# The last 64 rows of two weight matrices, loaded as two halves instead of one interleaved load

## The chip, the core and the metric

The kernel runs on one core of one Trainium2 chip. A core has a matrix engine (TensorE, PE in the profile; its weight loads are listed as PEld), three engines for vectors and scalars (VectorE or DVE, ScalarE or ACT, GpSimd or POOL), a SyncE (SP) that issues transfers here, and 16 DMA engines that carry them out. On-chip memory (SBUF) has 128 partitions. The metric is the device time of one execution in microseconds (us), median of several runs. Before the change it is 1147.22 us (3 runs, 1147.13 to 1147.64).

## The reference

Two kinds of layer alternate, A B A B, on eight batch rows of one token each, with D = 448 features:

```
A: q = norm(x) @ wq                       # wq: 448 x 4096, 16 heads of 256
   scores = q k^T / 16, softmax over 4096 keys, o = p v   # 8 kv heads, two q heads each
   x = x + o @ wo                         # wo: 4096 x 448
B: y = norm(x)
   x1 = y + shift(gelu(norm(y) @ w1)) @ w2
   x = x + x1 + gelu(norm(x1) @ w3) @ w4  # w3: 448 x 1792, w4: 1792 x 448
```

The shift moves features along the token axis; as there is one token, all that it moves in is padding, so its term is zero and w1 and w2 are never read. Both A layers read the same weights and the same caches. k_cache and v_cache are bf16 of 8 x 8 x 4096 x 256, 2 MB for each batch row and head, in all 128 MiB each.

## The kernel before, in words

**Tiling.** Weights stay in SBUF through the whole kernel. The contraction over D = 448 rows is cut into blocks of 128, 128, 128 and 64 rows, one block on the partitions at a time. The block with 64 rows is *packed*: its columns 0 to n/2 lie on partitions 0 to 63, its columns n/2 to n on partitions 64 to 127, so that it takes n/2 columns of SBUF in place of n (`packed`, lines 402 to 409; `packed_ap`, line 426, finds a column again). The right-hand side of the product has the last 64 features once on partitions 0 to 63 (slot 3) and once, copied in line 478 or 894, on 64 to 127 (slot 4), with zeros on the other half. `packed` is called for wq (line 411, n = 4096, 8 KB rows) and for w3 (line 533, n = 1792, 3.5 KB rows). wo and w4 have one load each (lines 530 and 534); w4's pieces are rows of 448 numbers.

**K and V.** SBUF has 30 slots of 4 KB on each partition for K and V (512 KB a slot). A K load fills two slots (1 MB; line 666), a V load one (line 741). DVE transposes K in place in 32-bit blocks (line 672), PE makes the scores (line 688), DVE, POOL and ACT the softmax (lines 696 to 722), PE the product with V (PV, line 752), and after a small transpose and combination (lines 757 to 774) PE multiplies by wo (line 782). With the last head of a batch row comes its `tail`: residual, two norms, w3 (line 810), gelu, w4 (line 835), residual, and in layer 0 the norm and q projection for the second A layer (line 492).

**Order.** The first A layer of batch row b runs next to the second of row b - 1. Some K blocks are kept in their slots from the first to the second (`KEPT`; for row 0 nine K loads, 18 of the 30 slots), and all other K and all V are read twice. The order of transfers is written by `load_order`; all of them are issued by SP, in one queue: x, then wq, then K and V of row 0 with wo after twelve K loads, then w3 and w4 after row 0's V, then row 1. `Graph.schedule` plays the kernel forward with durations and priorities given by hand, and with one modelled DMA queue of a fixed rate, and so fixes one static order for each engine. A semaphore stands for each slot and for each weight transfer; a consumer waits for those it needs. SP waits before an issue until the slot that it will fill is free; else it issues ahead.

**Where the change lies.** Lines 407 to 409: the fourth load of a packed weight. Its target is all 128 partitions, and its source is a view of the 64 rows with the half `u` as the first of three dimensions (2 x 64 x n/2). The first consumer of wq is the q projection of all eight rows at the start (PE, line 492, after `norm`, whose last instruction is line 478); of w3, the tail of row 0.

Of the kernel before, what the change touches and what calls it, by code (L numbers as in the profile page):

```python
# [6 lines left out]
P = 128  # L7
B = 8
D = 448
# [265 lines left out]
def bass_interleave_layers__gqa_block_cached__mixer_s_mlp__decode_kernel(  # L275
# [66 lines left out]
    def res(name, psum=False):  # L342
        if name not in R:
            R[name] = Res(psum)
        return R[name]
# [7 lines left out]
    def dma(fn, nbytes, prio, queue=dma_order, **kw):  # L353
        t = g.add("sp", fn, 0.0, prio, **kw)
        t.nbytes = nbytes
        queue.append(t)
        return t
# [44 lines left out]
    def packed(w_sb, w, n, name, queue):  # L402

        for c in range(3):
            dma(lambda e, c=c: e.dma_start(w_sb[:, c * n:(c + 1) * n], w[c * P:(c + 1) * P, :]),
                P * n * 2, 0, queue, writes=[res(name)])
        dma(lambda e: e.dma_start(w_sb[:, 3 * n:3 * n + n // 2],
                                  w[3 * P:D, :].rearrange("r (u f) -> u r f", u=2)),
            64 * n * 2, 0, queue, writes=[res(name)])

    packed(wq_sb, A_wq, HQ * DH, "wq", dma_order)

    def xin(e):
# [87 lines left out]
    def expand(layer, b, prio):  # L501
# [13 lines left out]
        for a in range(4):  # L515
            def cp(e, a=a):
# [14 lines left out]
                              A_wo.rearrange("(h m k) n -> m h (k n)", m=P, k=4)),  # L531
        D * 4096 * 2, 0, late, writes=[res("wo")])
    packed(w3_sb, B_w3, F, "w3", late)
    dma(lambda e: e.dma_start(w4_sb[:, 0:NFT * D].rearrange("p (t n) -> p t n", n=D),
                              B_w4.rearrange("(t m) n -> m t n", m=P)),
# [366 lines left out]
    for layer in range(2):  # L902
        d = {}
        for nm in ("n2", "n3"):
# [6 lines left out]
          writes=[res("xb0"), res("xb1"), res("xc0"), res("xc1")])  # L911
# [65 lines left out]
    for e in ("pe", "dve", "act", "pool"):  # L977
        n = 0
# [9 lines left out]
    for t in everything:  # L988
        e = t.chosen
# [94 lines left out]
```

## Time and profile before

| | us |
|---|---|
| median of 3 runs | 1147.22 |
| the profiled execution | 1147.47 |
| its span, first to last instruction | 1145.7 |
| DVE busy in the span | 770.8 (67%) |
| PE busy in the span | 700.3 (61%) |
| ACT, POOL busy | 114.5, 98.2 |

The span holds 41,855 instructions. DMA moves 452.63 MB, 395 GB/s over the span, almost all on the queue that SP issues to. 512 V loads and 163 K loads make nearly all of it.

A row of a table of stretches gives a stretch from A to B in us from the span's start, its length, the busy time (and number of instructions) of PE, PEld, DVE, ACT and POOL, the granted clock of PE as a share of full speed, the mean busy share of the 16 DMA engines (a little above 1 where transfers on one engine overlap), and the GB/s that they moved. A row in order of time gives start, duration, engine, line, operation, output <- input, and, in brackets, how long the engine had been idle and what ended that. For a DMA issued by SP (SPq), the duration is that of the issue on SP and not of the transfer.

### The profile page before, as it was taken

How to read it: one execution, taken by the hardware profiler on the slowest of the kernel's cores; microseconds unless marked ns; L12 is line 12 of the kernel's file. 1: busy time of each engine (PE TensorE's matmuls, PEld its weight loads, DVE VectorE, ACT ScalarE, POOL GpSimd, SP SyncE). 2: the span in 40 equal slices, each digit the busy share in tenths (PEclk: the TensorE clock that was granted, in tenths of full speed). 3: DMA queues.
4: the chain of work that ended last, by engine and by line, in shares of the span. 5: the costliest groups of instructions: out<-in, count | busy, mean ns of one | idle time of the engine just before them, and what ended most of it. 6: DMA issues, size and time to landing. Idle time of an engine off the chain costs nothing.

```text
span 1145.7 us, 41855 instructions
## 1 busy us (share of the span) xinstructions
PE 700.3 (61%) x18716; PEld 465.1 (41%) x18716; DVE 770.8 (67%) x2704; ACT 114.5 (10%) x434; POOL 98.2 (9%) x269
## 2 busy tenths in 40 slices
PE   0435465586556855577555775568555676557765
PEld 0322354244432544335443454335443355333553
DVE  2855589645995369943897449954699538974463
ACT  0100012101110011100111011100111001110110
POOL 0000011001110011100111001100111001110010
PEclk9999986557555565555555555555655555555655
DMA  9999899999999999999999999999999999999993
GB/s 300 415 386 371 309 401 415 411 403 407 414 414 399 403 415 415 412 398 397 414 415 408 402 407 415 414 400 401 416 414 413 396 399 416 414 407 403 405 407 150
DMA packets 101384, 452.63 MB, mean 395 GB/s; under 512 B 10948, under 2 KB 12884, under 8 KB 79956
## 3 DMA queue, kind: packets, MB, share of 16 engines
q1 hardware_dynamic: 101188, 449.96, 98.2%
q8 instruction: 146, 2.39, 0.9%
q14 instruction: 34, 0.28, 0.1%
q10 hardware_dynamic: 16, 0.01, 0.0%
HBM read 449.91 MB, written 0.01 MB: 393 GB/s over the span
## 4 chain that ended last, share of the span: by engine, by line
DMA 36%; DVE 35%; PE 20%; issue 7%; SPq 1%; ACT 1%; ACTq 0%; DVEq 0%
DMA kv<-in_A_v_cache_dram 30%; DVE kv L672 22%; PE psO L752 7%; PE psS L688 6%; DMA kv<-in_A_k_cache_dram 5%; DVE psX L711 2%; DVE small L696 2%; PE psM L492 2%; PE psM L782 2%; DVE oX L757 1%; DVE oT L771 1%; DVE small L884 1%; PE psO L764 1%; PE psM L810 1%; DVE small L698 1%
## 5 line engine op out<-in xcount | busy, mean ns | idle before, releaser
L672 DVE STREAM_TRANSPOSE kv<-kv 128x512 int32<-128x512 int32 x652 | 431.2, 690 | 32.8 <-DMA kv<-in_A_k_cache_dram 32.6
L688 PE MATMUL psS<-kv,qx 128*8 128x128 bf16 x8192 | 253.1, 295 | 178.6 <-DVE kv L672 83.0
L752 PE MATMUL psO<-kv,ring 128*2 128x256 bf16 x4096 | 290.2, 397 | 105.3 <-DMA kv<-in_A_v_cache_dram 89.5
L688 PEld LDWEIGHTS psS<-kv,qx 128*8 128x8 bf16 x8192 | 194.5, 114 | 238.2 <-DVE kv L672 113.1
L752 PEld LDWEIGHTS psO<-kv,ring 128*2 128x2 bf16 x4096 | 80.5, 93 | 180.5 <-DMA kv<-in_A_v_cache_dram 144.6
L757 DVE STREAM_TRANSPOSE oX<-psO 128x256 f32<-128x256 f32 x128 | 56.2, 439 | 110.2 <-PE psO L752 109.6
L700 POOL PARTITION_ALL_REDUCE small<-small x128 | 46.6, 364 | 726.2 <-DVE small L698 719.0
L782 PE MATMUL psM<-oT,wo_sb 128*128 128x1 bf16 x2048 | 74.3, 166 | 53.6 <-DVE oT L771 39.9
L706 ACT ACTIVATE psX<-psS,small 128x256 f32<-128x256 f32 x128 | 57.4, 448 | 455.3 <-DVE small L702 411.1
L696 DVE TENSOR_REDUCE small<-psS 128x1 f32<-128x256 f32 x128 | 52.4, 409 | 70.4 <-PE psS L688 53.3
L782 PEld LDWEIGHTS psM<-oT,wo_sb 128*128 128x128 bf16 x2048 | 64.1, 104 | 83.0 <-DVE oT L771 64.2
L771 DVE TENSOR_SCALAR oT<-psO,small 64x4 bf16<-64x4 f32 x256 | 55.4, 216 | 47.3 <-PE psO L764 42.7
L720 POOL PARTITION_ALL_REDUCE small<-small x128 | 51.4, 401 | 272.5 <-DVE small L718 237.8
L711 DVE STREAM_TRANSPOSE psX<-psX 128x256 f32<-128x256 f32 x128 | 57.6, 450 | 11.8 <-ACT psX L706 10.3
L764 PE MATMUL psO<-oX,id 128*32 128x4 f32 x1024 | 36.9, 201 | 28.1 <-DVE oX L757 21.2
L764 PEld LDWEIGHTS psO<-oX,id 128*32 128x32 f32 x1024 | 30.6, 147 | 46.0 <-DVE oX L757 36.6
L835 PE MATMUL psM<-small,w_sb 128*128 128x1 bf16 x896 | 30.1, 166 | 23.8 <-DVE small L827 23.7
L835 PEld LDWEIGHTS psM<-small,w_sb 128*128 128x128 bf16 x896 | 26.9, 104 | 38.6 <-DVE small L827 29.0
L715 ACT CAST ring<-psX 128x64 bf16<-128x64 f32 x128 | 27.2, 213 | 149.3 <-DVE psX L711 149.3
L492 PEld LDWEIGHTS psM<-small,wq_sb 128*128 128x128 bf16 x1024 | 30.7, 104 | 17.2 <-issue 12.0
L810 PE MATMUL psM<-small,w_sb 128*128 128x1 bf16 x896 | 28.8, 166 | 10.9 <-DVE small L894 6.7
L492 PE MATMUL psM<-small,wq_sb 128*128 128x1 bf16 x1024 | 34.2, 166 | 2.0 <-DVE small L894 1.8
(91 smaller groups left out, 354.1 us busy)
## 6 DMA issues: line engine op xcount, KB each, us to landing
kv<-in_A_v_cache_dram SPq DMA_DIRECT2D x512, 512.0 KB, 9.1
kv<-in_A_k_cache_dram SPq DMA_DIRECT2D x163, 1024.0 KB, 19.1
wo_sb<-in_A_wo_dram SPq DMA_DIRECT2D x1, 3584.0 KB, 27.9
wq_sb<-in_A_wq_dram SPq DMA_DIRECT2D x3, 1024.0 KB, 7.0
w_sb<-in_B_w_dram SPq DMA_DIRECT2D x1, 1568.0 KB, 21.3
w_sb<-in_B_w_dram SPq DMA_DIRECT2D x3, 448.0 KB, 15.3
wq_sb<-in_A_wq_dram SPq DMA_DIRECT2D x1, 512.0 KB
w_sb<-in_B_w_dram SPq DMA_DIRECT2D x1, 224.0 KB
```

Source lines behind the costliest of these rows:

```text
L492: last = e.matmul(M[:, base + col * nb:base + (col + 1) * nb], w, xn[:, :, kx], start=(k == 0), stop=(k == NCC - 1))
L672: return e.transpose(ap, ap)
L688: last = e.matmul(S[32 * j:32 * j + 8, w * y:w * y + w], qx[x][:, h, 2 * c + u, :], kt[:, :, c, 8 * j:8 * j + 8, u], start=(c == 0 and u = ...
L696: g.add("dve", lambda e: e.tensor_reduce(pm[par][:, :], S[:, 0:256], axis=AX.X, op=ALU.max), (0.46, 0.33), pr, reads=[rS], writes=[res(f"p ...
L706: g.add("act", lambda e: e.activation(p_ps.rearrange("p (z k y) -> p y z k", z=8, k=8), S[:, 0:256].rearrange("p (y z k) -> p y z k", y=4, ...
L711: g.add("dve", lambda e: e.transpose(p_ps, p_ps), (0.48, 0.38), pr, reads=[rP], writes=[rP])
L752: last = e.matmul(O[32 * j:32 * j + 2, 0:DH], ring[:, pin.slot, i, 2 * a:2 * a + 2], slot_ap(vin)[:, i * DH:(i + 1) * DH], start=(a == 0 a ...
L757: g.add("dve", lambda e: e.transpose(oX[:, :].rearrange("p (c r) -> p c r", r=32), O[:, 0:DH].rearrange("p (a r k) -> p a k r", a=2, k=4)) ...
L764: last = e.matmul(O[32 * a:32 * a + 32, 256:260], id4[:, :], oX[:, :].rearrange("p (a k r) -> p a k r", a=2, k=4)[:, a % 2, :, a // 2], st ...
L771: g.add("dve", lambda e, j=j: e.tensor_scalar(oT[64 * j:64 * j + 64, jb, 4 * h:4 * h + 4], O[64 * j:64 * j + 64, 256:260], rc_ring[64 * j: ...
L782: last = e.matmul(psM[layer][:, c:c + 1], wo_sb[:, c0:c0 + P], oT[:, jb, kt_:kt_ + 1], start=(first and k == 0 and c == 0), stop=False, sk ...
L835: last = e.matmul(M[:, 64 + c:65 + c], w4_sb[:, c0:c0 + P], hT[:, ft:ft + 1], start=(ft == 0), stop=(ft == NFT - 1))
```

## The change

The fourth load of each packed weight is taken apart by halves. Each of the two new loads brings 64 rows of n/2 columns to 64 partitions: the first to partitions 0 to 63, the second to 64 to 127. The same bytes go to the same places, in two issues of SP in place of one, each with its own semaphore. The planner sees two transfers of half the bytes. This is done for wq (256 KB each) and w3 (112 KB each).

```diff
         for c in range(3):
             dma(lambda e, c=c: e.dma_start(w_sb[:, c * n:(c + 1) * n], w[c * P:(c + 1) * P, :]),
                 P * n * 2, 0, queue, writes=[res(name)])
-        dma(lambda e: e.dma_start(w_sb[:, 3 * n:3 * n + n // 2],
-                                  w[3 * P:D, :].rearrange("r (u f) -> u r f", u=2)),
-            64 * n * 2, 0, queue, writes=[res(name)])
+        for u in range(2):
+            dma(lambda e, u=u: e.dma_start(w_sb[64 * u:64 * u + 64, 3 * n:3 * n + n // 2],
+                                           w[3 * P:D, u * n // 2:(u + 1) * n // 2]),
+                32 * n * 2, 0, queue, writes=[res(name)])
```

## The prediction

> **What bounds the kernel now.** I read the page first: the slices, the chain that ended last and the DMA issues.
>
> ```profile
> DMA  9999899999999999999999999999999999999993
> GB/s 300 415 386 371 309 401 415 411 403 407 414 414 399 403 415 415 412 398 397 414 415 408 402 407 415 414 400 401 416 414 413 396 399 416 414 407 403 405 407 150
> ...
> DMA 36%; DVE 35%; PE 20%; issue 7%; SPq 1%; ACT 1%; ACTq 0%; DVEq 0%
> ...
> wq_sb<-in_A_wq_dram SPq DMA_DIRECT2D x3, 1024.0 KB, 7.0
> w_sb<-in_B_w_dram SPq DMA_DIRECT2D x1, 1568.0 KB, 21.3
> ...
> wq_sb<-in_A_wq_dram SPq DMA_DIRECT2D x1, 512.0 KB
> w_sb<-in_B_w_dram SPq DMA_DIRECT2D x1, 224.0 KB
> ```
>
> The DMA engines are busy from the start to the last slice, at about 410 GB/s, except in slices 1 and 5 (300 and 309). A slice is 28.6 us: slice 1 holds the load of wq, slice 5 (114 to 143 us) follows that of w3. The last two lines are the two loads that the change splits; they alone among the weights have no time to landing.
>
> Then a table of stretches; its columns are start and end, length, busy time of the five engine rows, the clock, the DMA share and GB/s.
>
> ```profile
> 2.50:11.60 9.10, 0.00 (x0) 0.00 (x0) 1.36 (x13) 0.00 (x0) 0.52 (x3) 1.00 0.96 397
> 11.60:27.60 16.00, 1.54 (x8) 1.28 (x8) 4.13 (x27) 0.00 (x0) 0.62 (x3) 1.00 1.01 280
> 27.60:71.50 43.90, 20.52 (x600) 14.23 (x600) 34.83 (x86) 5.19 (x16) 3.40 (x9) 1.00 1.02 412
> 71.50:83.50 12.00, 3.24 (x80) 1.68 (x80) 6.24 (x17) 1.37 (x6) 1.16 (x3) 1.00 0.95 357
> 83.50:109.50 26.00, 12.58 (x320) 7.64 (x320) 13.51 (x31) 0.78 (x3) 0.76 (x2) 1.00 1.02 412
> 109.50:126.50 17.00, 7.41 (x134) 3.26 (x127) 8.46 (x42) 1.39 (x5) 0.76 (x2) 1.00 0.57 174
> 126.50:145.50 19.00, 9.85 (x322) 9.01 (x326) 13.09 (x46) 0.99 (x4) 0.54 (x2) 1.00 1.00 406
> 145.50:160.00 14.50, 9.30 (x300) 7.07 (x292) 11.44 (x34) 2.05 (x8) 1.33 (x4) 1.00 0.98 390
> 160.00:1130.00 970.00, 629.67 (x16834) 416.11 (x16828) 669.39 (x2371) 102.02 (x392) 88.59 (x235) 0.54 1.01 407
> 113.50:117.50 4.00, 2.44 (x48) 0.94 (x48) 0.88 (x3) 0.00 (x0) 0.00 (x0) 1.00 0.13 53
> ```
>
> From 160 us on nothing is left over: share 1.01 for 970 us, while DVE is busy 669 of 970 (69%) and PE 630 (65%). The end is therefore set by when the DMA engines get through their 450 MB. The last row is the key: for 4 us, 0.13 of 16 engines worked, that is two, at 53/2 = 26.5 GB/s each, the same as the 412/16 = 25.8 of one engine in the full stretches. Two engines had a backlog; fourteen had nothing.
>
> Last, the order of time around those stretches, and the end of the chain.
>
> ```profile
> 18.66 0.17 DVE L478 COPY w_sb<-w_sb 64x8 bf16<-64x8 bf16 x1
> 28.17 3.56 PE L492 MATMUL psX<-w_sb,wq_sb 128*128 128x8 bf16 x128 [12.34 <-DMA wq_sb<-in_A_wq_dram]
> 30.33 1.90 DVE L672 STREAM_TRANSPOSE kv<-kv 128x512 int32<-128x512 int32 x3 [11.49 <-DMA kv<-in_A_k_cache_dram]
> 109.26 8.41 SPq L534 DMA_DIRECT2D w_sb<-in_B_w_dram  x1
> 117.72 10.30 SPq L666 DMA_DIRECT2D kv<-in_A_k_cache_dram  x5
> 133.02 0.71 DVE L672 STREAM_TRANSPOSE kv<-kv 128x512 int32<-128x512 int32 x1 [4.03 <-DMA kv<-in_A_k_cache_dram]
> 137.20 0.33 SPq L666 DMA_DIRECT2D kv<-in_A_k_cache_dram  x1
> ...
> 1114.81 15.08 DMA kv<-in_A_v_cache_dram
> ```
>
> The normed input is ready at 18.83 us, yet the q projection starts at 28.17 (waiting for wq) and the first K transpose at 30.33. I read the backlog as the work of line 407: its source has the half (two of them) as its outermost dimension, and the load is dealt to two engines. The Trainium skill has that rule: DMA: Bandwidth & Descriptors, "Why a DMA increments its semaphore by 16 and not by 1", says that the engine count is the largest number up to 16 that divides the slowest dimension of both sides, so 2 here and 16 for a half with 64 rows; the trace agrees with the 2 (share 0.13), and no row of before shows the 16.
>
> **The change part by part.** *The wq load.* 512 KB (524,288 B) on two engines is 262 KB each, 262/25.8 = 10.2 us; on sixteen it is 524/412 = 1.3 us. Every K load behind it has a share on the two engines and lands only with them. Beyond this backlog all sixteen were slower while it ran: 280 GB/s over 16.0 us against 412 just after. Lost there: 16.0 x (1 - 280/412) = 5.1 us. That the load slows the others is inferred: the rate is 397 before it and 412 after it. From both sides: 0 to 5.1; I take 5.1, since the 412 follows with the same K loads in the queue.
>
> *The lag carried on.* At 71.5 to 83.5 engines run dry for want of issues: 12.0 x (1 - 357/412) = 1.6 us. I put it down to slots freed late because the two engines deliver late.
>
> *The w3 load and w4 behind it.* 224 KB on two engines is 115/25.8 = 4.4 us each, on top of what is left of the first lag. The issue of w4 stands 8.41 us in SP's queue, and five K loads another 10.3. That is the 0.13 row: w4's data has not begun, so I read SP's queue as held by the two engines' full rings. 174 GB/s x 17.0 us is 2.96 MB, of which w4 is 1.61. At 412 the rest, 1.35 MB, takes 3.3 us. For w4, whose rows are shorter (896 B), 412 GB/s gives 3.9 us; 313, measured at 120 to 124 us beside the w3 load, gives 5.1; I take 4.5 between them. Lost: 17.0 - 3.3 - 4.5 = 9.2 us (8.6 to 9.8).
>
> *What it adds.* Two issues in place of one for each weight. SP took 0.36 to 0.43 us for a wq block and 0.64 for the load that goes, so about 0.2 us more; behind it stand the first five K loads, whose data starts only when the engines finish wq at 11.6 us, so that 8 us of queue cover it. At w3, rings are full and an issue lasts as long as the drain. Each of the PE groups that waits for a weight gets one more semaphore to test, early in the kernel, with DMA as the bound: 0. The planner sees two tasks of half the bytes on one modelled queue, so the second ends when the one ended; I expect the order kept, slot numbers at most changed. POOL and ACT queues are not touched.
>
> *The price of a load to 64 partitions* no row shows. Nearest is the wq block to 128 partitions at 397 GB/s: cost 0. As if only half the engines' rate were to be had (206 GB/s), 524 + 229 KB cost 3.6 us in place of 1.8, so 1.8 more. A gain below 0 is excluded, as these bytes cannot go faster than the full stretches. Nothing decides, so I take 0.9. On this the Trainium skill speaks against the change: SBUF — State Buffer, "Door 1: The DMA port swizzle", says partitions 0 to 63 reach half of the sixteen ports; by its asymptote of 218 GB/s I estimate 1.6 us more, and no run here shows it.
>
> **Does the compute let it through?** After wq the first K would land at 11.6 + 1.3 + 2.5 (1 MB at 412) = 15.4 us, and DVE is free at 18.83, so the q projection and the transposes move 9 to 11 us up. Batch 0's last PV (117.83) waits on the two engines; it moves by 8.9 (10.2 - 1.3) + 5.1 = 14 us, to 104. From it to SP's next free slot (K load issued at 137.20) are 19.4 us, 4.0 of them DVE's wait for the late K: so 15.4, and the issue falls at about 119. The loads issued ahead of it (five K, two V, 6.3 MB, 15.3 us) follow w4, which would land at about 112 to 115, and last to 127 or later: the queue does not run dry. After that everything is the same sequence, earlier, with DMA still the bound and the same 16 us from the last V (1129.9) to the end.
>
> Sum: 5.1 + 1.6 + 9.2 - 0.9 = 15.0 us. The profiled execution took 1147.47 (span 1145.7, 1.8 around it): 1132.5; against the median of 1147.22, 0.25 less: 1132.2, say 1132. If the stretches from 126.5 to 160 also fill up (0.3 + 0.8), and 9.8 and 0 hold, the gain is 17.6; with 8.6 and 1.8 lost, it is 13.5. Own range 1129 to 1134.
>
> **The rivals.** *The slow start is K's own* (strided K rows at the start of a run): then 5.1 stays, the gain is 9.9, 1137.3. For it: the stretch holds K loads alone. Against: the rate is 412 from the instant that q projection can start. Chance 0.10.
>
> *Given back at the slots.* Kept K blocks fill 18 of 30 slots until layer 1 of batch 0. If its tail moves only as far as the first compute, 9.3 us (28.17 to 18.83), DMA runs dry before 160 us and the gain is 9.3: 1137.9. For it: SP's 8 us wait before 137.20. Against: the 15.4 worked out above, DVE at half load before 130. Chance 0.09.
>
> *Nothing changes:* two loads to separate halves run as late as one did; 1147.2. The same page of the Trainium skill, under "Can I just issue two DMAs to hit both halves?", says that they serialize; it speaks of sixteen engines on both sides, so what it would take is the 0.9 to 1.8 above, and the 0.13 row is against more. Chance 0.04.
>
> *Slower:* each half is dealt to one engine, and both to the same one. Then its backlog doubles, 20.3 and 8.9 us in place of 10.2 and 4.4: 14.6 more, 1161.8. It decides below two engines for a half; at two it is even. For it: no row shows a half. Against: all 128-partition loads ran on sixteen. Chance 0.03.
>
> **How the numbers follow.** The main case has 0.74. Measurements here tell 0.2% (2.3 us) from no change. Faster: 0.74 + 0.10 + 0.09 = 0.93; same 0.04; slower 0.03. The range 1128.5 to 1138 holds the main case nearly whole, with 0.5 us below for what later stretches may do, and both partial cases: about 0.85.
>
> **What would show it.** Right: the stretch 11.6 to 27.6 at about 410 GB/s; q projection near 19 us; first transpose near 19; no stretch with a DMA share of 0.13; w4 landed near 112 to 115; the last V near 1115; both halves with an ordinary time to landing. Wrong: 280 GB/s still there from 11.6 (the first rival), shares well below 1 between 115 and 160 with SP waiting on PE (the second), or the q projection still at 28 us (the third) or later (the fourth). A shift at 160 us that shrinks again by the end would say that DMA isn't the bound throughout.

## The result, and the profile after

The changed kernel takes 1133.5 us (median of 4 runs, 1133.38 to 1133.89) against 1147.18 us (4 runs, 1146.98 to 1147.64): a ratio of 0.9881, 95% interval 0.9864 to 0.9898, 13.7 us less. The profiled execution took 1133.89 us, its span 1132.1. The static order of every compute engine is the same as before; SP's list differs only in the two loads that became two issues each.

The page of the changed kernel, the slices and the DMA issues:

```profile
DMA  9999999999999999999999999999999999999993
GB/s 344 415 412 394 411 417 412 405 384 417 415 412 402 404 415 415 403 404 409 415 414 400 402 413 415 413 397 401 416 415 413 395 410 413 416 395 407 409 408 135
...
wq_sb<-in_A_wq_dram SPq DMA_DIRECT2D x2, 256.0 KB, 11.6
w_sb<-in_B_w_dram SPq DMA_DIRECT2D x2, 112.0 KB, 14.7
```

Slice 1 went from 300 to 344 GB/s and slice 5 from 309 to 411; slices 3, 4 and 6 rose too. From the seventh on they lie between 384 and 417 GB/s in both kernels, but for the last. The halves now have a time to landing (11.6 and 14.7 us).

The table of stretches of the changed kernel, columns as before (start and end, length, busy time of the five engine rows, clock, DMA share, GB/s):

```profile
2.50:11.60 9.10, 0.00 (x0) 0.00 (x0) 1.35 (x13) 0.00 (x0) 0.20 (x1) 1.00 0.98 370
11.00:15.00 4.00, 0.95 (x6) 0.78 (x6) 1.13 (x9) 0.00 (x0) 1.14 (x5) 1.00 1.01 225
11.60:15.60 4.00, 0.95 (x6) 0.78 (x6) 1.63 (x12) 0.00 (x0) 0.93 (x4) 1.00 1.00 257
11.60:27.60 16.00, 5.67 (x164) 5.24 (x168) 9.56 (x37) 1.80 (x3) 0.93 (x4) 1.00 1.01 376
27.60:71.50 43.90, 19.17 (x536) 12.14 (x524) 35.42 (x94) 4.75 (x18) 4.56 (x12) 1.00 1.02 413
71.50:83.50 12.00, 5.48 (x136) 3.39 (x136) 4.14 (x9) 0.00 (x0) 0.00 (x0) 1.00 1.02 414
83.50:105.00 21.50, 11.67 (x264) 5.89 (x264) 12.75 (x36) 2.16 (x8) 1.51 (x4) 1.00 1.02 410
105.00:115.00 10.00, 4.56 (x102) 3.16 (x102) 5.08 (x28) 0.00 (x0) 0.00 (x0) 1.00 1.07 372
115.00:130.00 15.00, 7.53 (x241) 6.78 (x241) 12.32 (x44) 0.78 (x3) 0.36 (x1) 1.00 1.01 418
160.00:1114.00 954.00, 618.19 (x16534) 410.01 (x16522) 654.57 (x2326) 99.56 (x382) 86.01 (x228) 0.54 1.02 408
```

No stretch has a low DMA share any more. The rate is below 400 only around the halves: 370 from 2.5 to 11.6 (397 before), 257 in the four microseconds after 11.6, and 372 at 105 to 115. The body, 408 GB/s at a share of 1.02, is as it was.

The changed kernel in order of time, and the last wait of its chain (the lines after the change are numbered one higher than before):

```profile
19.34 1.30 DVE L673 STREAM_TRANSPOSE kv<-kv 128x512 int32<-128x512 int32 x2
19.37 0.78 PE L493 MATMUL psX<-w_sb,wq_sb 128*128 128x8 bf16 x23 [3.06 <-DVE w_sb L479]
...
95.62 1.96 SPq L408 DMA_DIRECT2D w_sb<-in_B_w_dram  x2
97.62 0.85 SPq L535 DMA_DIRECT2D w_sb<-in_B_w_dram  x1
98.52 14.51 SPq L667 DMA_DIRECT2D kv<-in_A_k_cache_dram  x5
106.33 0.60 PE L753 MATMUL psO<-kv,ring 128*2 128x256 bf16 x8 [0.66 <-DMA kv<-in_A_v_cache_dram]
122.37 0.33 SPq L667 DMA_DIRECT2D kv<-in_A_k_cache_dram  x1
...
1099.98 16.34 DMA kv<-in_A_v_cache_dram
```

The q projection starts at 19.37 in place of 28.17, released by the norm (DVE, line 479) and no longer by wq; the first transposes start at 19.34 in place of 30.33. SP is through with w4's issue in 0.85 us in place of 8.41. Batch 0's last PV is at 106.33 (117.83 before), the late K issue at 122.37 (137.20), and the last V load's PV at 1099.98 + 16.34, 1116.3 (1129.9). So these events come 9 to 15 us earlier in the first 130 us, and 13.6 us are left at the end.

### The profile page after: what moved, and what is told of

It reads as the page before. It is cut to its first block, busy times and chain, and to the rows that moved or that the text cites. A ratio compares the mean times of both kernels' runs of the same rounds, so it can differ in the third digit from the quotient of the medians.

```text
span 1132.1 us, 41859 instructions
## 1 busy us (share of the span) xinstructions
PE 698.0 (62%) x18716; PEld 466.5 (41%) x18716; DVE 770.5 (68%) x2704; ACT 114.5 (10%) x434; POOL 98.3 (9%) x269
## 4 chain that ended last, share of the span: by engine, by line
DVE 35%; DMA 32%; PE 23%; issue 8%; ACT 1%; SPq 0%; POOL 0%; POOLq 0%; ACTq 0%; DVEq 0%
DMA kv<-in_A_v_cache_dram 28%; DVE kv L673 21%; PE psO L753 8%; PE psS L689 7%; PE psM L493 3%; DMA wo_sb<-in_A_wo_dram 2%; DVE psX L712 2%; DVE small L697 2%; PE psM L783 2%; DMA kv<-in_A_k_cache_dram 2%; DVE oX L758 1%; PE psO L765 1%; DVE oT L772 1%; DVE small L885 1%; PE psM L811 1%
## 5 line engine op out<-in xcount | busy, mean ns | idle before, releaser
L673 DVE STREAM_TRANSPOSE kv<-kv 128x512 int32<-128x512 int32 x652 | 431.1, 690 | 16.7 <-DMA kv<-in_A_k_cache_dram 16.4
L689 PEld LDWEIGHTS psS<-kv,qx 128*8 128x8 bf16 x8192 | 196.9, 115 | 243.8 <-DVE kv L673 118.4
L836 PEld LDWEIGHTS psM<-small,w_sb 128*128 128x128 bf16 x896 | 27.0, 104 | 37.7 <-DVE small L828 27.6
## 6 DMA issues: line engine op xcount, KB each, us to landing
w_sb<-in_B_w_dram SPq DMA_DIRECT2D x1, 1568.0 KB, 18.1
w_sb<-in_B_w_dram SPq DMA_DIRECT2D x3, 448.0 KB, 16.4
wq_sb<-in_A_wq_dram SPq DMA_DIRECT2D x2, 256.0 KB, 11.6
w_sb<-in_B_w_dram SPq DMA_DIRECT2D x2, 112.0 KB, 14.7
```

The lines of the kernel that those rows point to most:

```text
L673: return e.transpose(ap, ap)
L689: last = e.matmul(S[32 * j:32 * j + 8, w * y:w * y + w], qx[x][:, h, 2 * c + u, :], kt[:, :, c, 8 * j:8 * j + 8, u], start=(c == 0 and u = ...
L836: last = e.matmul(M[:, 64 + c:65 + c], w4_sb[:, c0:c0 + P], hT[:, ft:ft + 1], start=(ft == 0), stop=(ft == NFT - 1))
```

## The experiments

**Each load alone.** The two halves for wq only, and for w3 only:

```diff
-        dma(... one load, source "r (u f) -> u r f" ...)
+        if name == "wq":          # the other kernel: "w3"
+            for u in range(2):
+                dma(... half u to partitions 64 * u to 64 * u + 63 ...)
+        else:
+            dma(... one load, source "r (u f) -> u r f" ...)
```

> Only wq's last rows are loaded as two halves; w3 keeps the interleaved load. Theory (two engines carry the interleaved load, and the lag of wq's is still there when w3's comes): the slow start (5.1 us), the thin stretch (1.6) and the carried lag go; w3's own lag (4.4 us of work on two engines against 0.6 shared, 3.8 more) stays, so 5.4 of the 9.2 us at w4 go too. Half loads cost the 1.5 us that the changed kernel shows at 11.6 to 15.6 us. 1147.2 - 5.1 - 1.6 - 5.4 + 1.5 = 1136.6 us. Rival (the 9.2 us at w4 come from w3's load alone): 1147.2 - 6.7 + 1.5 = 1142.0, with a stretch of 0.13 DMA share as long as before.

> Only w3's last rows are loaded as two halves; wq keeps the interleaved load. Theory: the slow start and the thin stretch stay, the lag of wq's load is still there at 110 us, and only w3's own 3.8 us go, less 0.6 for two half loads: 1144.0 us; q projection at 28 us as before. Rival (the stall at w4 is w3's alone): all of 9.2 us goes, 1138.6.

Measured: wq alone 1134.4 us (ratio 0.9885, 0.9871 to 0.9900), w3 alone 1144.4 us (0.9974, 0.9964 to 0.9985), beside 1147.6. Expected were 1136.6 and 1144.0, so wq alone gave 2.2 us more than thought. The gains are 13.2 and 3.2; together they would make 16.4, and the change as a whole gave 13.7. The two loads share a loss: the 9.2 us at w4 need the lag that wq's load left. Stretches around w3 and w4, first of the kernel with wq's halves, then of the one with w3's:

```profile
105.00:110.00 5.00, 2.39 (x48) 0.91 (x40) 0.99 (x5) 0.00 (x0) 0.00 (x0) 1.00 1.05 370
110.00:115.00 5.00, 1.59 (x33) 1.43 (x34) 3.31 (x21) 0.00 (x0) 0.00 (x0) 1.00 1.00 285
97.22 7.37 SPq L540 DMA_DIRECT2D w_sb<-in_B_w_dram  x1
```

```profile
115.00:120.00 5.00, 2.90 (x48) 0.91 (x48) 0.84 (x3) 0.00 (x0) 0.00 (x0) 1.00 0.60 214
119.00:121.00 2.00, 0.84 (x19) 0.29 (x12) 0.89 (x3) 0.00 (x0) 0.00 (x0) 1.00 0.13 53
120.00:125.00 5.00, 1.73 (x30) 1.39 (x30) 2.46 (x16) 0.00 (x0) 0.00 (x0) 1.00 0.56 184
109.69 0.59 SPq L540 DMA_DIRECT2D w_sb<-in_B_w_dram  x1
110.33 13.79 SPq L672 DMA_DIRECT2D kv<-in_A_k_cache_dram  x5
```

With wq's lag gone, w3's interleaved load no longer empties the engines (share 1.00 at 110 to 115), although w4's issue still takes 7.37 us on SP. The stretch 105 to 115 moves 328 GB/s against 372 in the changed kernel, which is worth 1.1 us. The times differ by 1 us at most (1134.4 beside 1133.4 to 1134.2 in the runs of the changed kernel), and their intervals overlap, so the runs don't show that splitting w3 as well brought anything; I had left 3.8 us for it.

With wq's lag kept, a stall comes although w3 is split and w4 is issued in 0.59 us. From 119 to 121 us the share is 0.13 again, two engines at work alone. The only source left in this kernel whose outermost dimension is two is that of wq's load, issued at 2.5 us: its backlog is still there more than 100 us later. A long issue alone is not the sign of this. The five K loads stand in SP's queue for 13.79 us here and for 14.51 in the changed kernel, whose engines are busy all the while; what counts is whether fourteen engines run out of work meanwhile. So the stall comes from the backlog of wq's load, and it falls on whichever issue comes when the others are done. The rival that made w4's stall w3's own is refuted by both (1142.0 and 1138.6 expected).

**Four engines.** The same bytes in two loads whose sources have an outermost dimension of four:

```diff
+        for u in range(2):
+            dma(lambda e, u=u: e.dma_start(w_sb[:, 3 * n + u * n // 4:3 * n + (u + 1) * n // 4],
+                w[3 * P + 32 * u:3 * P + 32 * u + 32, :].rearrange("r (v f) -> v r f", v=4)), ...)
```

> The last 64 rows in two loads of 32 rows, each to 128 partitions, from a source whose outermost dimension is a quarter of the columns (four of them). The same bytes, but other numbers on the partitions than the products want, so that the projections by wq and w3 are not the reference's; nothing else is changed. Theory (the outermost dimension of the source sets the number of engines, here four): wq's backlog is 131 KB, 5.1 us an engine against 1.3 shared, w3's 2.2 against 0.6; the excess is 3.8 + 1.6 = 5.4 us against 8.9 + 3.8 = 12.7 before, and if the loss goes with it, 15.9 x 5.4/12.7 = 6.8 us are lost: 1147.2 - 9.1 = 1138.1. Rival (it is the one load with its 128 partitions and interleaved source, however dealt): as before, 1147; rival (the split in two issues is what helps): 1133.

Measured: 1140.1 us (0.9936, 0.9921 to 0.9951), a gain of 7.5 where 9.1 was expected. The stretches and the q projection of this kernel:

```profile
11.60:27.60 16.00, 5.40 (x152) 4.97 (x152) 8.10 (x34) 0.14 (x1) 0.68 (x3) 1.00 1.01 311
105.00:110.00 5.00, 2.94 (x55) 0.96 (x56) 1.92 (x7) 0.99 (x4) 0.40 (x1) 1.00 0.75 301
110.00:115.00 5.00, 2.59 (x54) 1.01 (x51) 0.89 (x3) 0.00 (x0) 0.00 (x0) 1.00 0.53 171
109.00:112.00 3.00, 2.13 (x40) 0.71 (x32) 0.44 (x2) 0.00 (x0) 0.00 (x0) 1.00 0.26 105
21.50 3.56 PE L493 MATMUL psX<-w_sb,wq_sb 128*128 128x8 bf16 x128 [5.59 <-DMA wq_sb<-in_A_wq_dram]
```

The time lies between the two kernels, and so does the q projection (21.50, between 19.37 and 28.17). The row from 109 to 112 us shows the engines themselves: a share of 0.26 is four of sixteen, at 105/4 = 26 GB/s each, where the kernel before had two. Two issues to 128 partitions with a source of four parts are neither as before nor as the change: what counts is the number of parts outermost. That number is the engine count by the rule of the Trainium skill that the prediction weighed (DMA: Bandwidth & Descriptors, on the increment by 16); this run agrees with it.

**Two parts, other rows.** Is it the reading of one row by two engines that slows all sixteen?

```diff
-                                  w[3 * P:D, :].rearrange("r (u f) -> u r f", u=2)),
+                                  w[0:2 * P, 0:n // 2].rearrange("(u x r) f -> u x r f", u=2, x=2)[:, 0]),
```

> One load as before, again with an outermost dimension of two, but its two parts are rows 0 to 63 and rows 128 to 191 (the first half of the columns of each), so that no row is read by both; the last contraction block of wq and w3 then holds other numbers than it should. Theory (two engines, whatever they read): 1147 as before, q projection at 28 us, and 280 GB/s from 11.6 to 27.6. Rival (the whole core is slowed because two engines read the halves of the same rows): the 5.1 us of the slow start go, the backlog stays: 1142, and over 350 GB/s from 11.6 us on.

Measured: 1147.5 us (1.0001, 0.9992 to 1.0011), and from 11.6 us the same 280 GB/s:

```profile
11.60:27.60 16.00, 1.55 (x8) 1.28 (x8) 4.12 (x27) 0.00 (x0) 1.13 (x5) 1.00 1.02 280
```

Taking both halves of the same rows has no price; an outermost dimension of two has. Why two engines with a backlog slow the other fourteen isn't shown by this.

**One load that uses all engines.** The source can be walked with the row outside and the half inside; the 128 pieces then follow one another in memory and make one dimension:

```diff
-                                  w[3 * P:D, :].rearrange("r (u f) -> u r f", u=2)),
+                                  w[3 * P:D, :].rearrange("r (u f) -> (r u) f", u=2)),
```

> One load of all 128 partitions, whose source has the row outside and the half inside (row 0 left half, row 0 right half, row 1 left half ...): 128 pieces in one dimension, so that nothing but the assignment of pieces to partitions differs; the last contraction block of wq and w3 then meets the wrong features. Theory (two engines were the whole harm, and a load to 64 partitions runs at half rate): sixteen engines and full rate, so the stretch 11.6 to 15.6 us, 257 GB/s in the changed kernel, goes to about 410 (1.5 us), the one at w3 gains 0.6 or more: 1131.0 to 1131.5. Rival (loads to 64 partitions cost nothing, and the 1.3 us by which the gain fell short lie elsewhere): 1133.5. Rival (splitting in two issues is what helped): 1147.

> The changed kernel once more, as the measure for the three beside it: 1133.5 us, a ratio of 0.988 to the kernel before.

Measured beside each other: 1130.6 us (0.9852, 0.9837 to 0.9867), the changed kernel 1133.4 (0.9878, 0.9861 to 0.9894); 2.8 us apart, with ranges of 1130.4 to 1131.1 and 1133.3 to 1134.1 that don't meet, though the two intervals against the kernel before overlap. The same stretches as above, in the kernel with one load:

```profile
2.50:11.60 9.10, 0.00 (x0) 0.00 (x0) 1.35 (x13) 0.00 (x0) 0.27 (x2) 1.00 0.96 388
11.60:15.60 4.00, 0.95 (x6) 0.78 (x6) 1.69 (x12) 0.00 (x0) 0.86 (x4) 1.00 1.02 432
11.60:27.60 16.00, 5.75 (x168) 5.33 (x172) 9.65 (x37) 1.80 (x3) 0.86 (x4) 1.00 1.02 421
105.00:115.00 10.00, 3.38 (x86) 2.96 (x86) 6.07 (x34) 0.21 (x1) 0.00 (x0) 1.00 1.05 406
130.00:160.00 30.00, 17.33 (x604) 13.84 (x604) 26.86 (x82) 5.28 (x20) 4.62 (x13) 0.84 1.01 415
```

432 in place of 257 where the last rows of wq arrive, and 406 in place of 372 where those of w3 do. So loads to 64 partitions are slow, and the change pays for them. Splitting was no help in itself: one load does better than two. SBUF — State Buffer in the Trainium skill ("Door 1: The DMA port swizzle") has 64 partitions at half the rate of 128; the 225 GB/s of the changed kernel from 11 to 15 us are near half of 412 and agree with that rate. How much time it costs doesn't follow from it, as told below.

**Can the two halves be made to overlap?** Two tries that keep the layout: four loads of 32 rows, issued left, right, left, right; and wq's halves issued by ACT at the start, beside the wq blocks on SP.

```diff
+        for q in range(4):                      # first kernel
+            u, r = q % 2, 32 * (q // 2)
+            dma(lambda e, u=u, r=r: e.dma_start(w_sb[64 * u + r:64 * u + r + 32, 3 * n:3 * n + n // 2], ...
+        if e == "act":                          # second kernel, in the order of issues
+            for t in on_act:
+                t.ops[0](eng).then_inc(t.sem[0], 16)
```

> The halves cut once more, into four loads of 32 rows to 32 partitions, issued left, right, left, right, so that each load is followed by one to the other half of the partitions. Same layout, same result. If half-rate comes from the partitions that a load reaches and the engines run out of step, loads to both halves overlap: 1132.5. If the engines move in step, as the changed kernel: 1133.5. If each more issue costs (0.6 us apiece on SP), 1134.5.

> The changed kernel, with wq's two half loads issued from ACT's queue at the start, beside the three wq blocks on SP's, w3 as in the changed kernel. Theory (half rate by partitions): pieces of the halves alternate with pieces to 128 partitions, so part of the 1.3 to 1.5 us lost at 11.6 to 15.6 us comes back: 1132.5. Rival (an engine carries the same bytes in any order): 1133.5.

Measured: 1133.1 us (0.9873, 0.9858 to 0.9887) and 1134.1 us (0.9882, 0.9867 to 0.9896), against the changed kernel's 1133.4: no difference that these runs can tell. That all of the 2.8 us come back is excluded; a few tenths are not. Four issues in place of two had no price either. In the second, the loss has only moved to where the halves now run:

```profile
2.50:11.60 9.10, 0.00 (x0) 0.00 (x0) 1.35 (x13) 0.00 (x0) 0.00 (x0) 1.00 0.99 317
11.60:15.60 4.00, 0.95 (x6) 0.78 (x6) 1.33 (x11) 0.00 (x0) 1.13 (x5) 1.00 1.00 418
```

(317 in place of 370 ahead of 11.6 us, 418 in place of 257 after it.)

**The one load with the reference's result.** The one load with the products made to fit it: the weights of row 384 + r lie on partitions 2r and 2r + 1, so the last 64 features have to be spread to pairs of partitions. After each norm PE does that with one small product, and DVE zeroes the odd or the even ones:

```diff
-        ops.append(lambda e: e.tensor_copy(dsts[-1][64:128, :, 4:5], dsts[-1][0:64, :, 3:4]))
+        g.add("pe", lambda e: e.matmul(M[:, 24:25], twice[0:64, :], dsts[-1][0:64, 0, 3:4], start=True, stop=True),
+              (0.4, 0.2), prio, reads=[dst_res, res("own")], writes=[rM])
+        g.add("dve", lambda e: e.tensor_scalar(dsts[-1][:, 0, 4:6], parity[:, :], M[:, 24:25], None, ALU.mult),
+              (0.21, 0.12), prio, reads=[rM, res("own")], writes=[dst_res])
```

> The one load of 128 rows by pieces (row 0 left half, row 0 right half, row 1 left half ...), made whole: after each norm PE spreads the last 64 features to pairs of partitions with one small product, and one DVE operation zeroes the odd or the even ones, in place of DVE's copy; the result is the reference's again. Theory (the loads set the time, and the spreading lies beside other work except in the last tail): one128's 1130.6 plus 0.5 us at the end, 1131.1, some 2 us under the changed kernel. Rival (each of the eight tails of layer 0 and 1 is on the path): 16 x 0.5 more, 1139.

> The changed kernel once more, on the same chip and in the same hour as the version beside it, as its measure: 1133.4 us, ratio 0.988.

Measured: 1133.9 us (0.9876, 0.9860 to 0.9893) beside 1134.2 (0.9881, 0.9866 to 0.9896): the load's gain was given back. The last tail in order of time:

```profile
1121.82 0.18 PE L903 MATMUL psM<-small,twice 64*128 64x1 bf16 x1 [2.43 <-DVE small L901]
...
1123.71 0.22 DVE L909 SCALAR_TENSOR_TENSOR small<-small,xT 128x4 f32<-128x4 f32 x1
1123.85 0.23 DVE L905 TENSOR_SCALAR small<-small,psM 128x2 bf16<-128x2 f32 x1
1124.14 1.66 PE L818 MATMUL psM<-small,w_sb 128*128 128x1 bf16 x56 [2.13 <-DVE small L905]
```

The small product is done at 1122.0, but DVE works through the second residual's operations (up to line 909) before line 905 finishes the input that w3's product waits for: 1.8 us lost at the end of the kernel. With a dependency that puts line 905 first:

```diff
-            g.add("dve", ops2[1:], ..., reads=[rL, src_res], writes=[xn_res], whole=whole)
+            g.add("dve", ops2[1:], ..., reads=[rL, src_res, dst_res], writes=[xn_res], whole=whole)
```

> The paired version with one order changed: the eight DVE operations that prepare the second residual now stand behind the one that finishes the product's input; in the version before they stood ahead of it and held the product with w3 up in the last tail, from 1121.80 to 1123.71 us. Theory (the load is worth its 2.8 us, and that wait was most of what the tail gave back): the last tail 1.8 us shorter, and 1.0 at 130 to 160 us too if row 0's tail was held up the same way: 1131.5, ratio 0.986. Rival (the added product and its two hand-overs cost what the load brings, in whatever order): 1133.9.

> The changed kernel once more, on the same chip and in the same hour as the version beside it, as its measure: ratio 0.988 to the kernel before, as in the earlier runs (1133.4 to 1134.2 us).

Measured: 1131.7 us (1131.49 to 1131.99; ratio 0.9857, 0.9841 to 0.9874) beside the changed kernel's 1133.75 (1133.47 to 1135.74; 0.9878). 2.0 us less, with ranges that don't meet, though the two intervals against the kernel before overlap. The load's 2.8 us are not all had: at 130 to 160 us the rate rose from 393 to 404 GB/s with the new order, where the kernel with one load has 415. The same lines are now:

```profile
1120.68 0.24 DVE L905 TENSOR_SCALAR small<-small,psM 128x2 bf16<-128x2 f32 x1 [0.28 <-PE psM L903]
1120.98 1.65 PE L818 MATMUL psM<-small,w_sb 128*128 128x1 bf16 x56 [0.33 <-DVE small L905]
```

## Why the prediction was right

1132 us was forecast, in a range of 1128.5 to 1138, and 1133.5 measured. The mechanism was right; one term of the sum, the price of a load to 64 partitions, was too small. Point by point:

- **What bounds the kernel** (the DMA engines to the last V load): right. From 160 us on both kernels move 407 to 408 GB/s at a share of 1.01 to 1.02, and what was gained at the start was there at the end.
- **Two engines carry the interleaved load**: right. Four parts give a time between and a stretch with four engines at work (share 0.26), one dimension of 128 the best time, and two parts of other rows the old one.
- **The slow start, 5.1 us**: it goes away with the load (376 GB/s in place of 280, and 421 with one load of 128 partitions), which refutes the rival that made it K's own. With two engines the low rate lasts until the q projection can start (28.17, 28.25 and 28.45 us in three kernels), with four until 21.50. Up to there only this load differs, so the load is the cause; how it slows K is not shown.
- **The thin stretch, 1.6 us**: right, 414 GB/s in place of 357.
- **The stall at w4, 9.2 us**: right in sum, as no stretch with a low share is left. That it needs the carried lag was argued, and the kernels with one split each show it. With wq's lag gone, w3's own part was 1.1 us at 105 to 115, not the 3.8 that its 4.4 us on two engines would give.
- **Added issues**: right at no cost, though not in size: SP took 1.34 us for both halves of wq, 0.7 more than for the one load and not 0.2, while the engines stayed full (share 0.98 from 2.5 to 11.6).
- **Price of a load to 64 partitions, 0.9 us in a bound of 0 to 1.8**: this term of the sum was mis-sized. It measured 2.8 us, the distance to the one load of 128 partitions. That is also one issue in place of two, but four issues took no longer than two. Against that kernel the stretches place it: 0.4 us at 2.5 to 11.6 (9.1 x (388 - 370)/412), 1.7 at 11.6 to 27.6 (16 x (421 - 376)/412) and 0.8 at 105 to 115 (10 x (406 - 372)/412), 3.0 in all, near the 2.8. The bound counted only the halves' own bytes at half rate. For wq that is 1.3 us (524 KB at 206 in place of 412 GB/s), and 2.1 were lost there, so what moves beside the halves must lose as well; why is not shown.
- **The later stretches, up to 1.1 us, left out of the sum**: with one load they move 415 GB/s at 130 to 160, in place of 406. The whole gain with one load is 17.0 us (1147.59 to 1130.58), against 15.9 + 1.1 worked out without the port term. That these agree so closely is partly luck, as the term for w4 alone was uncertain by 0.6 either way. The forecast of 15.0 took 0.9 from 15.9; the measured gain is 17.0 less 2.8, 14.2 in those runs (13.7 in the first). The port term was 1.9 us too small, and the 1.1 left out made up for more than half of that. That the total came out so near is luck to this extent.
- **Compute lets it through**: right; the late K issue fell at 122.37 (119 forecast) and the DMA share stayed at 1.01 or more around it. The last PV of batch 0 moved 11.5 us, not 14, for the price just told; it was of no consequence.

The signposts came as told: q projection near 19 us, no stretch at 0.13, landings for both halves, last V at 1116 (1115 forecast); w4 landed at 97.62 + 18.1 = 115.7, a little after the 112 to 115. Only the stretch 11.6 to 27.6 was at 376 in place of 410, which is the mis-sized term seen directly. The rivals of no change and of one engine for each half fell with the result, and so did the gain given back at the slots: the share stays at 1.01 from 115 to 160 us.

## What to carry to other kernels

A load that shows no time to landing, or a stretch whose DMA share is a small fraction such as 0.13, may be running on few engines: look at the outermost dimension of its source (the one that these runs varied), and write the same bytes so that it is long (128 here, or 64) instead of 2. In this queue, which nearly all loads share, the lag of a few engines didn't heal by itself: the loads behind it landed late, and 100 us later an issue was held while fourteen engines had nothing to do. Where a load can keep both the long outermost dimension and all 128 partitions, that is better than splitting it, and if the consumer has to be adapted, look at what stands between the adapting operation and the product that waits for it.

## What the runs showed that was not expected

- A load of 512 KB on two engines lowered what all sixteen moved from 412 to 280 GB/s for as long as it ran, whichever rows it read. With four engines the rate was lower still, for a shorter time. A row from the middle of each, first of the kernel before, then of the one with four engines:

```profile
13.00:26.00 13.00, 1.20 (x5) 1.00 (x4) 3.80 (x25) 0.00 (x0) 0.00 (x0) 1.00 1.01 269
12.00:20.00 8.00, 1.54 (x8) 1.28 (x8) 4.12 (x27) 0.00 (x0) 0.43 (x2) 1.00 1.05 236
```

Shared by sixteen, that is 16.8 and 14.8 GB/s an engine. As an estimate from these rows, 262 KB on one engine then take 15.6 us and 131 KB take 8.9, about as long as the two slow stretches last; so the few engines seem to have been slowed like the others. The runs leave the cause open.

- Half loads to 64 partitions cost 2.8 us for 0.75 MB in all, in whatever order and from whichever queue they were issued (1133.1 and 1134.1 beside 1133.4).
- The two loads' losses were not additive: 13.2 and 3.2 us alone, 13.7 together.
